# Windowed attention and a two-layer network on one core: transfers merged, and the ordered list given a limit of eight DMAs in flight

## The chip, the cores and the metric

One core of a Trainium2 chip runs the program. The metric is the device time in microseconds of one execution. The kernel before took 888.34 us as the median of three runs (885.73, 888.34 and 893.09).

## What is computed

```python
def _attn_ref(q, k, v):                    # 8 batches, 8 heads, 576 positions, 64 wide
    scores = scale * np.matmul(q, k.transpose(0, 1, 3, 2))
    mask = (rel >= 0) & (rel < 64)         # each position sees itself and the 63 before it
    ...                                    # softmax: minus the maximum, exp, over the sum + 1e-09
    return np.matmul(attn, v)

def _moe_ref(x, w_in, w_out):              # x: 4608 x 512, w_in: 512 x 2048, w_out: 2048 x 512
    h = x @ w_in
    g = np.maximum(0.01 * h, h)
    return g @ w_out
```

The attention's result, laid out as 4608 rows of 512, is the x of the network.

## The kernel before

**Tiles.** Queries are taken in blocks of 64 positions and two blocks at a time, called a pair, m = 0 to 35. A pair has scores of 128 keys by 2 x 512 columns, in two halves j = 0 and 1. The network runs over chunks of 512 rows. All products use values split into two parts (a high part in the matmul's own precision and the remainder), and three matmuls of 128 x 128 by 128 x 512 for each product, which are the parts of TensorE's work that the profile shows as m, h, acc, y and z.

**Stages.** First the string ORDER lists pairs 0 to 7, the conversion of the weights and the first products, word by word. The rest is built as a list of entries by op(engine, us, function, what it waits for, rank, lag, land). The function arrange then walks that list like a scheduler: each engine takes, among its entries whose predecessors have ended by the planned times, the one with the lowest rank, and the order that comes out is the order in which the instructions are issued. The planned times serve for nothing else. Everything on an engine runs in that order, so an instruction that waits holds all that stand behind it on its engine.

After ORDER come chunk products with tiles h and acc (early_first, early_second; lines 880 and 889), then three rounds s = 0, 1, 2. A round has a first product in seven half-size products (m, line 1058) and a second product: for s = 0 in the plain form (y, line 1083), for s = 1 and 2 again in seven half-size products (z, line 1121). In between them the attention of pairs 8 to 35 goes on, up to about 630 us.

**One late pair.** attend(m) loads q, k and v by DMAs that ScalarE issues (lines 161, 165 and 169), makes the scores on TensorE (line 272), adds the mask on VectorE, takes the maximum over the partitions on GpSimd (line 672), subtracts it, takes exp on ScalarE and sums over the partitions on GpSimd (line 675) into late_o. normalise(m) brings the sums into 128 x 8 numbers by two small DMAs (late_c, line 686), adds 1e-9 on ScalarE (690), inverts them on VectorE (694), writes them to HBM (rows, 697), and reads them back spread over the partitions (late_r, 710): half j's row of 512 goes to partitions 64 j to 64 j + 63. The product with V is on TensorE (722), the multiplication by late_r on VectorE (733) into late_n, and keep_of (736) writes that to x_rows in HBM. x_build (830, 835, 854, 857) reads two pairs back and makes the inputs of m.

**DMAs.** GpSimd issues those that fill a ring of four weight tiles (fill, line 1042); SyncE and ScalarE issue all others. Each of SyncE's and ScalarE's DMAs is given one of eight semaphores, by turns over both engines in the order of the list, and the engine that issues it first waits until the DMA that had the semaphore before has landed. No entry of the list says so: it is added when the program is built. The planned time of such an entry ends with its landing (land) only for those that wait for it.

**Stored weights.** split stores the single-precision copy of each half tile in w_single (line 241); store (632) puts the split parts into w_first and w_second. prepare(n, f) reads two singles, makes sums and differences of them on VectorE (979), splits these (982, 985) and stores them (989, 992): for n = 0 into w_first, for n = 1 into w_second, which holds eight blocks for the second products. In the second product y, high and low (1073, 1076) split one 128 x 512 tile of the activations at a time into one of four places; in z, wide_high and wide_low (1103, 1107) split 128 x 1024.

Of the kernel before, what the change touches and what calls it, by code (L numbers as in the profile page):

```python
# [24 lines left out]
P = 128  # L25
# [13 lines left out]
PACE = 2  # L39
EARLY = 20  # L40
FIRST_LATE = 14
# [61 lines left out]
def band_attention_ffn(ctx: ExitStack, tc: tile.TileContext, qT, kB, vW, vL, w_in, w_out, eye_mask, out, outT):  # L103
# [37 lines left out]
    qs = [const.tile([P, UNITS, NP, QB], F32, name=f"q{i}") for i in range(2)]  # L141
    ks = [const.tile([P, UNITS, NP, QB], F32, name=f"k{i}") for i in range(2)]
# [16 lines left out]
    def load_q(m, queue=nc.sync):  # L159
        if m < NU // 2:  # L160
            queue.dma_start(q_of(m), qT[m])

    def load_k(m, queue=nc.sync):
        if m < NU // 2:
            queue.dma_start(k_of(m), kB[m])
# [24 lines left out]
    w_single = dram.tile([2 * FT, P, 512], F32, name="w_single")  # L190
    w_first = dram.tile([P, half * 7 * 512], F32, name="w_first")
    w_second = dram.tile([P, 8 * half * 512], F32, name="w_second")
    second_at = w_second.rearrange("p (k f c) -> p k f c", k=8, f=half)
# [45 lines left out]
    def split(n):  # L239
        nc.scalar.copy(flat(parts(n)[0]), singles[n])  # L240
        nc.scalar.dma_start(w_single[n], singles[n])
# [238 lines left out]

    def idle(n):
# [14 lines left out]
    nc.scalar.dma_start(k_of(0), kB[0])  # L496
# [21 lines left out]
    def load(fn, *after, rank=1.0, us=0.5, land=4.0):  # L518
        return op("SP", us, fn, *after, rank=rank, land=land)

    def bulk(fn, *after, rank=1.0):
        return op("ACT", 0.45, fn, *after, rank=rank, lag=1.5, land=6.0)

    def arrange():
# [9 lines left out]
        order = []  # L534
        while any(waiting.values()):
            best = None
            for e, xs in waiting.items():
                if xs:
                    t = max(free[e], min(r for r, _ in xs))
                    if best is None or t < best[0]:  # L540
                        best = t, e
            t, e = best
            r, x = min((y for y in waiting[e] if y[0] <= t), key=lambda y: (y[1]["rank"], y[1]["n"]))
# [50 lines left out]
    def g_pair(n):  # L594
        t = pairs_of_g[n % 2] if n % 4 < 2 else own(("g", n // (2 * FT)), F32R)[:, n % 2]
        return t[:, 0], t[:, 1]

# [14 lines left out]
    for name in late.split():  # L612
# [3 lines left out]
        if kind == "raw":  # L616
            o["raw"] = bulk(partial(fetch_w, n), weights_of.get(n - 3, {}).get("join"), rank=0.2)
# [12 lines left out]

    def store(to, f, *cut):
        nc.sync.dma_start(to, both[f][cut])

    stored = []
    for f in turn_of:
        near, far = f % half, f // half
        for a, k in ((0, 0), (256, 4)) if far == 0 else ((256, 5),):
            to = first_at(near, k).rearrange("p (i c) -> p i c", i=2)
            stored.append((f, partial(store, to, f, slice(None), slice(2), slice(a, a + 256))))
        for a in range(2):  # L640
            to = second_at[:, (0, 2)[far] + (6, 2)[far] * a, near].rearrange("p (i c) -> p i c", i=2)
            stored.append((f, partial(store, to, f, slice(None), slice(2, 4), slice(256 * a, 256 * a + 256))))


# [50 lines left out]

    def rows_of(m):
# [11 lines left out]
    def spread_of(m, j):  # L708
        row = rows[m : m + 1, 512 * j : 512 * j + 512]
        nc.sync.dma_start(later["r"][64 * j : 64 * j + 64], row.broadcast_to([64, 512]))  # L710
# [20 lines left out]
    def product_of(m):  # L731
        x = by_unit(done_of(m)) if early(m) else turned(probs[m, "v"])
        nc.vector.tensor_tensor(by_unit(done_of(m)), x, turned(later["r"]), ALU.mult)
# [16 lines left out]
    at = {}  # L750

    def attend(m, gate):

        o, late = at.setdefault(m, {}), 0.0 if early(m) else 0.5
        before, two, three = (at.get(m - i, {}) for i in (1, 2, 3))
        if m > PAIRED:
# [3 lines left out]
            o["v"] = bulk(partial(load_v, m, nc.scalar), before["X1"])  # L760
# [3 lines left out]
        o["S"] = op(  # L764
            "PE", 1.0, partial(scores_of, m), o.get("q"), o.get("k"), before.get("E1"), before.get("E0"), three.get("take"), *takes, s_free,
# [3 lines left out]
        for j in range(2):  # L769
            free = (three.get("V"), three.get(f"A{j}"))  # L770
            o[f"E{j}"] = op("DVE", ONE, partial(shield_of, m, j), o["S"], *(() if held else free), gate, before.get("E1"), rank=0.8 + late)
            o[f"C{j}"] = op("ACT", ACTS, partial(copy_of, m, j), o[f"E{j}"], *free, rank=0.5 + late) if held else o[f"E{j}"]
        for j in range(2):
            o[f"P{j}"] = op("POOL", 1.95, partial(max_of, m, j), o[f"C{j}"], before.get(f"B{j}"), rank=0.5 + late)
            o[f"B{j}"] = op("DVE", ONE if held else TWO, partial(minus_of, m, j), o[f"P{j}"], rank=0.8 + late)
            o[f"X{j}"] = op("ACT", ACTS, partial(exp_of, m, j), o[f"B{j}"], rank=0.8 + late)
        for j in range(2):
            o[f"A{j}"] = op("POOL", 3.5, partial(add_of, m, j), o[f"X{j}"], before.get(f"c{j}"), rank=0.4 + late)
            o[f"c{j}"] = load(partial(compact_of, m, j), o[f"A{j}"], two.get("rows"), rank=0.3 + late)

    def normalise(m):

        late = 0.0 if early(m) else 0.5
# [3 lines left out]
        guard = op("ACT", 0.22, partial(guard_of, m), o["c0"], o["c1"], rank=0.8 + late, lag=0.3 + 6 * late)  # L787
        o["I"] = op("DVE", 0.25, partial(inverse_of, m), guard, rank=0.4 + late)
        o["rows"] = load(partial(rows_of, m), o["I"], rank=0.3 + late)
        for j in range(2):  # L790
            if m + 2 in at:
                at[m + 2][f"c{j}"]["after"].append(o["rows"])
        spread = [load(partial(spread_of, m, j), o["rows"], before.get("Y"), rank=0.3 + late) for j in range(2)]
        if early(m):
            free = [after["E1"], before.get("take"), o["I"]]
# [6 lines left out]
        o["Y"] = op("DVE", TWO if early(m) else ONE, partial(product_of, m), *spread, o.get("take"), o["V"], *kept, rank=0.8 + late, lag=0.3 + 6 * late)  # L802
        if m < UPC // UNITS * LEAD:
            hi = op("ACT", ACTS, partial(high_early, m), o["Y"], *x2_free, rank=0.8 + late)
            o["kept"] = [op("DVE", TWO, partial(low_early, m), hi, rank=0.8 + late)]
# [9 lines left out]
    def x_build(s, n, xt_of, xt_free, x_free):  # L815

        urge, wait = (1.4, 2.6) if s else (0.2, 0.2)
# [11 lines left out]
        def fetch(i):  # L829
            nc.sync.dma_start(xt_of()[0][:, 512 * i : 512 * (i + 1)], x_rows[m + i])  # L830

        got = [load(partial(fetch, i), *at[m + i]["kept"], *xt_free, rank=urge) for i in range(2)]
# [69 lines left out]
    def reload_of(c):  # L902
        t = stage[c] = place("xb", F32, 2) if c else place("xa1", F32)
        for i in range(4 if c else 2):
            nc.sync.dma_start(t[:, 512 * i : 512 * (i + 1)], sums.pop((c, i)))

    def early_out(c, i):
# [3 lines left out]
        else:  # L911
            (nc.scalar.copy if i % 2 else nc.vector.tensor_copy)(o, acc[c, i])
        nc.sync.dma_start(out[c * CH + i * P : c * CH + (i + 1) * P, :], o)
# [4 lines left out]
    def second_step(n):  # L918
# [5 lines left out]
        if n in ends:  # L924
            evicted[c] = []
            for i in range(4):
                engine = "DVE" if c == 1 or c == 0 and i < 2 or i % 2 == 0 else "ACT"
                evicted[c].append(op(engine, 0.75, partial(early_out, c, i), seconds[n][i], *reloads[c], rank=0.1))

    for n, (c, f) in enumerate(walk):  # L930
# [16 lines left out]
        if n in ends:  # L947
            reloads[c] = [load(partial(reload_of, c), first, s_free, rank=0.1)] if c < 2 else [first]
# [18 lines left out]
    def prepare(n, f, at, hurry, *freed):  # L967
# [399 lines left out]
```

## Time and profile before

| what | value |
|---|---|
| median of three runs | 888.34 us |
| the profiled execution | 888.97 us |
| its span, first to last instruction | 887.2 us |
| granted TensorE clock, mean | 0.987 |
| TensorE busy | 853.5 us, 96% of the span |
| VectorE busy | 631.6 us, 71% |
| ScalarE busy | 376.0 us, 42% |
| GpSimd busy | 364.2 us, 41% |
| moved by DMA | 227.08 MB, mean 256 GB/s |

Busy time is the union of an engine's instructions; those that only issue a DMA or wait are not in it. In the rows of the profile PE is TensorE, PEld its weight loads, DVE VectorE, ACT ScalarE, POOL GpSimd and SP SyncE; ACTq and SPq stand for the issuing of a DMA on these engines. A name such as L1058 is a line of the kernel before. Behind a row of instructions "[5.91 <-DVE gs L900]" says how long the engine sat idle before them and what ended that.

### The profile page before, as it was taken

Reading aid. Unit: us, or ns where it says so; the run is one execution under the profiler, and the core shown is the slowest. Engines: PE = TensorE matmul, PEld = TensorE weight load, DVE = VectorE, ACT = ScalarE, POOL = GpSimd, SP = SyncE. Lnnn points to the kernel's source line nnn. Section 1 sums busy time; section 2 is a strip of 40 time slices with the busy share of each in tenths; the row PEclk is TensorE's granted clock in tenths of the full one; section 3 lists DMA queues with packets and bytes.
Section 4 is the critical chain, followed back from the end, with each engine's and each line's share of the span. In section 5 each row is a group of like instructions: output and inputs, shape, how many; then the busy total and the mean of one; then the engine's idle time right before and its main releaser. Section 6 shows DMA issues by size and latency. Waiting matters only on the chain.

```text
span 887.2 us, 16927 instructions
## 1 busy us (share of the span) xinstructions
PE 853.5 (96%) x6778; PEld 690.0 (78%) x6778; DVE 631.6 (71%) x891; ACT 376.0 (42%) x620; POOL 364.2 (41%) x218
## 2 busy tenths in 40 slices
PE   8999999999999997999999899989999999999998
PEld 5776888888777776888887678767888888888886
DVE  7889885768579864875776989466578864545863
ACT  4655554333333333544453534253354523334431
POOL 5323000958768720677776777663000100000000
PEclk9999999999999998999999999989999999999999
DMA  9875876786899997799999998976856776666662
GB/s 342 265 233 184 275 219 240 234 302 207 276 292 336 314 317 273 245 299 356 309 295 317 295 300 266 344 235 207 276 195 214 236 242 210 194 191 197 199 222 87
DMA packets 103742, 227.08 MB, mean 256 GB/s; under 512 B 17008, under 2 KB 47856, under 8 KB 94704
## 3 DMA queue, kind: packets, MB, share of 16 engines
q0 software_dynamic: 14432, 90.18, 31.5%
q10 hardware_dynamic: 41712, 77.31, 26.3%
q1 hardware_dynamic: 47520, 58.51, 20.3%
q8 instruction: 53, 0.87, 0.4%
q14 instruction: 25, 0.20, 0.1%
HBM read 168.59 MB, written 57.26 MB: 255 GB/s over the span
## 4 chain that ended last, share of the span: by engine, by line
PE 48%; DMA 12%; DVE 9%; issue 3%; ACT 1%; SPq 1%; ACTq 0%; POOL 0%; DVEq 0%
PE m L1058 25%; PE z L1121 17%; DMA w_second<-p 2%; DMA late_r<-rows 2%; DMA w_second<-pspare 2%; DMA rows<-late_c 2%; DMA x_rows<-late_n 1%; PE y L1083 1%; PE acc L889 1%; DMA p<-x_rows 1%; PE s L272 1%; PE o L722 1%; DMA outT<-p 1%; DVE p L835 1%; DVE gs L1076 1%
## 5 line engine op out<-in xcount | busy, mean ns | idle before, releaser
L1058 PE MATMUL m<-pfew,p 128*128 128x512 f32 x720 | 171.5, 393 | 0.8 <-DVE pxa L1067 0.7
L1058 PEld LDWEIGHTS m<-pfew,p 128*128 128x128 f32 x720 | 134.8, 189 | 30.2 <-DVE pxa L1067 1.1
L1042 POOL DMA_DIRECT2D p<-w_second x44 | 26.3, 597 | 143.0 <-PE z L1121 98.8
L889 PE MATMUL acc<-p,gs 128*128 128x512 f32 x324 | 79.8, 394 | 0.0
L1042 POOL DMA_DIRECT2D p<-w_first x42 | 22.8, 542 | 134.0 <-PE m L1058 78.6
L1058 PE MATMUL m<-pxb,p 128*128 128x512 f32 x288 | 72.1, 397 | 5.0 <-ACT p L1070 5.0
L672 POOL PARTITION_ALL_REDUCE g<-late_f x20 | 37.0, 1894 | 96.1 <-DVE late_f L657 71.6
L675 POOL PARTITION_ALL_REDUCE late_o<-late_f x20 | 65.5, 3283 | 20.5 <-ACT late_f L683 12.3
L1067 DVE TENSOR_TENSOR p<-m,pxa 128x512 f32<-128x512 f32 x60 | 41.3, 688 | 41.9 <-PE m L1058 41.6
L1067 DVE TENSOR_TENSOR pxa<-m,pxa 128x512 f32<-128x512 f32 x60 | 41.3, 689 | 41.0 <-PE m L1058 38.0
L889 PEld LDWEIGHTS acc<-p,gs 128*128 128x128 f32 x324 | 60.1, 188 | 13.0
L1070 ACT ACTIVATE p<-p 128x512 f32<-128x512 f32 x60 | 37.9, 631 | 74.2 <-DVE p L1067 74.1
L1058 PEld LDWEIGHTS m<-pxb,p 128*128 128x128 f32 x288 | 54.4, 191 | 17.3 <-ACT p L1070 5.4
L880 PE MATMUL h<-pxa,p 128*128 128x512 f32 x228 | 58.4, 405 | 5.9 <-DVE gs L900 5.9
L675 POOL PARTITION_ALL_REDUCE late_o<-late_e x18 | 58.9, 3292 | 12.5 <-ACT late_e L683 8.0
L675 POOL PARTITION_ALL_REDUCE late_o<-e x18 | 58.8, 3285 | 8.2 <-ACT e L683 5.7
L1121 PE MATMUL z<-gs,p 128*128 128x512 f32 x240 | 57.6, 389 | 0.0
L880 PEld LDWEIGHTS h<-pxa,p 128*128 128x128 f32 x228 | 43.9, 195 | 16.5 <-DVE gs L900 7.2
L1083 PE MATMUL y<-gs,p 128*128 128x512 f32 x192 | 48.7, 406 | 3.8 <-issue 3.8
L1121 PEld LDWEIGHTS z<-gs,p 128*128 128x128 f32 x240 | 45.0, 188 | 9.4
L1121 PE MATMUL z<-third,p 128*128 128x512 f32 x216 | 51.9, 389 | 0.0
L1121 PE MATMUL z<-pxa,p 128*128 128x512 f32 x216 | 51.9, 389 | 0.0
(192 smaller groups left out, 1710.2 us busy)
## 6 DMA issues: line engine op xcount, KB each, us to landing
p<-w_second POOLq DMA_DIRECT2D x44, 1024.0 KB, 5.3
p<-w_first POOLq DMA_DIRECT2D x42, 1024.0 KB, 6.1
w_single<-w ACTq DMA_DIRECT2D x32, 256.0 KB, 4.4
w_second<-pspare ACTq DMA_DIRECT2D x16, 512.0 KB, 6.0
raw<-w_out ACTq DMA_DIRECT2D x15, 512.0 KB, 4.4
k<-kB ACTq DMA_DIRECT2D x28, 256.0 KB, 4.7
raw<-w_in ACTq DMA_DIRECT2D x14, 512.0 KB, 4.3
more_v<-vL ACTq DMA_DIRECT2D x14, 512.0 KB, 4.4
```

Of the source, the lines that this page charges most:

```text
L272: nc.tensor.matmul(ps[j][t, c : c + QB], k[i][s, p], q[s, w, p], start=not begun and (not more or (w, p) == (0, 0)), stop=not begun and no ...
L672: nc.gpsimd.partition_all_reduce(most_of(j), e_of(m)[:, j], P, ReduceOp.max)
L675: nc.gpsimd.partition_all_reduce(sum_of(j), e_of(m)[:, j], P, ReduceOp.add)
L722: nc.tensor.matmul(ps[64 * j : 64 * j + 64, c : c + QB], v[:, 2 * p + j], e_of(m)[:, j, c : c + QB], start=True, stop=True,)
L880: nc.tensor.matmul(ps, a[:, k, :], b[:, k], start=i == 0, stop=i == len(terms) - 1)
L889: nc.tensor.matmul(acc[c, i], a[:, i * P : (i + 1) * P], b, start=begin and k == 0, stop=n in ends and k == 2)
L1042: nc.gpsimd.dma_start(to, of)
L1058: nc.tensor.matmul(tiles[b], w[:, 256 * i + 128 * kt : 256 * i + 128 * kt + 128], x_part(OF_X[k], j, kt), start=begin and c == 0, stop=c = ...
L1067: nc.vector.tensor_tensor(to(), tiles[b], x(), ALU.add)
L1070: nc.scalar.activation(to(), to() if b is None else tiles[b], AF.Prelu, alpha=0.01)
L1083: nc.tensor.matmul(tiles[i], a, b, start=f == 0 and k == 0, stop=f == FT - 1 and k == 2)
L1121: nc.tensor.matmul(tiles[b + i], a, x, start=begin and f == 0 and c == 0, stop=f == half - 1 and c == 2, skip_group_check=not begin,)
```

## The change

1. arrange now keeps eight landing times (LANES): an entry of SyncE or ScalarE with a landing can't start in the plan before the earliest of them. Planned landings become 4.8 and 6.5 us in place of 4.0 and 6.0, and several ranks change. The DMAs that send results (early_send, send) and the single reloads become entries of their own.
2. q and k lie in one input, qk, and from pair 10 on come in one load of 128 x 1024 (load_qk).
3. The inverse sums of a pair are spread by one DMA in place of two (spread_of), and x_build reads its two pairs by one.
4. Only the singles of w_in are stored. w_second now holds the split parts of w_out by f, stored by one DMA for each f in place of two; the sums and differences have a tensor of their own, w_sums. prepare(1, f) reads both parts from w_second and adds them (whole_of, a 128 x 1024 addition more on VectorE), and waits for these stores and for x_build(0). In z the factors that aren't sums are read from w_second in pieces of 256 numbers.
5. For pair 19 alone (direct) the inverse is taken on the whole tile: two additions of 1e-9 on ScalarE, one reciprocal of 128 x 512 on VectorE; its two small DMAs, the write and the spread are gone.
6. In y the activations are split 128 x 1024 at a time into one of two places, by wide_high and wide_low.

```diff
+LANES = 8
+DIRECT_FROM = 19
...
+    def load_qk(m):
+        nc.scalar.dma_start(both_qk[m % 2], qk[m])
...
     def split(n):
         nc.scalar.copy(flat(parts(n)[0]), singles[n])
-        nc.scalar.dma_start(w_single[n], singles[n])
+        if n % 2 == 0:
+            nc.scalar.dma_start(w_single[n // 2], singles[n])
...
-        order = []
+        order, landed = [], [0.0] * LANES
+
+        def begins(ready, x):
+            return max(ready, landed[0]) if x["land"] and x["engine"] != "POOL" else ready
...
-                    t = max(free[e], min(r for r, _ in xs))
+                    t = max(free[e], min(begins(*y) for y in xs))
...
+            if x["land"] and e != "POOL":
+                landed.pop(0)
+                landed.append(x["end"])
...
+    def whole_guard_of(m, j):
+        half_of = slice(64 * j, 64 * j + 64)
+        nc.scalar.activation(sum_of(0)[half_of], sum_of(j)[half_of], AF.Copy, bias=1e-9)
+
+    def whole_inverse_of(m):
+        nc.vector.reciprocal(sum_of(0), sum_of(0))
...
-    def spread_of(m, j):
-        row = rows[m : m + 1, 512 * j : 512 * j + 512]
-        nc.sync.dma_start(later["r"][64 * j : 64 * j + 64], row.broadcast_to([64, 512]))
+    def spread_of(m):
+        nc.sync.dma_start(later["r"], rows[m].rearrange("(j c) -> j c", j=2)[:, None].broadcast_to([2, 64, 512]))
...
-            if m > PAIRED + 1:
-                o["q"] = bulk(partial(load_q, m, nc.scalar), two["S"], rank=0.5 + late)
-            o["k"] = bulk(partial(load_k, m, nc.scalar), before["S"], rank=0.2 + late)
...
+        if m > PAIRED + 1:
+            o["k"] = bulk(partial(load_qk, m), before["S"], rank=0.2 + late)
...
-        got = [load(partial(fetch, i), *at[m + i]["kept"], *xt_free, rank=urge) for i in range(2)]
+        got = [load(fetch, *at[m]["kept"], *at[m + 1]["kept"], *xt_free, rank=urge, land=5.0)]
...
-            to = prep(0)[:, i::2] if n else prep(0)[:, 2 * i : 2 * i + 2]
-            nc.scalar.dma_start(to, w_single[2 * (f + half * i) + n].rearrange("p (k c) -> p k c", k=2))
+            if n:
+                to = tile_of()[:, 1024 * i : 1024 * (i + 1)].rearrange("p (j c) -> p j c", j=2)
+                nc.scalar.dma_start(to, w_second[:, f::half, 512 * i : 512 * (i + 1)])
+            else:
+                nc.scalar.dma_start(prep(0)[:, 2 * i : 2 * i + 2], w_single[f + half * i].rearrange("p (k c) -> p k c", k=2))
+
+        def whole_of():
+            nc.vector.tensor_tensor(prep(0), prep(0), prep(1), ALU.add)
...
+    used_last[0] = used_last[0] + x_done
+    for f in range(half):
+        prepare(1, f, 0, OUT_PREP + 0.1 * f, *used_last[0])
...
+    def factor(of, f):
+        if isinstance(of, int):
+            return w_sums[:, of, f : f + 4].rearrange("p f c -> p (f c)")
+        begin, a = of
+        return w_second[:, begin + f : begin + f + 4].rearrange("p f (i c) -> p (f i) c", i=2)[:, :, a : a + 256]
...
-                hi = op("ACT", ACTS, partial(high, q, partial(g_part, t, f)), made[t, f], *free, rank=0.2)
-                split_of[t, f] = op("DVE", TWO, partial(low, q, partial(g_part, t, f)), hi, rank=0.2)
+                    hi = op("ACT", 1.07, partial(wide_high, s, 2 * (q % 2), t, j, p), made[t, f], made[t, f + 1], *free, rank=0.2)
+                    lo = op("DVE", 1.6, partial(wide_low, s, 2 * (q % 2), t, j, p), hi, rank=0.2)
```

In all, ScalarE issues 165 DMAs in place of 207 and SyncE 262 in place of 322; GpSimd's 86 and TensorE's matmuls stay.

Three places of the order, word for word. The words in brackets are what a row waits for: DMAHW0 to DMAHW7 are the eight semaphores, the others are engines.

**ScalarE, the end of the chunk products.** L894 and L897 before (L933 and L936 now) take the tile h out of TensorE's bank and make its high part, which the products acc need. Before:

```order
L897 CAST gs0_81<-h2_7_3448 128x512 [waits PE_49,Activation_49]
L690 ACTIVATE late_c1_1789<-late_c1_1789 128x8 [waits DMAHW0_49]
L976 DMA pspare_18_1804<-w_single_96 128x2x256 [waits DMAHW7_49,DMAHW2_49]
L976 DMA pspare_18_1804<-w_single_96 128x2x256 [waits DMAHW3_49]
L992 DMA w_first_97<-p14_24_2971 128x1536 [waits DMAHW4_49]
L992 DMA w_first_97<-p14_24_2971 128x512 [waits DMAHW7_49]
L894 ACTIVATE h2_8_3490<-h2_8_3490 128x512 [waits DVE_49,PE_49]
L992 DMA w_first_97<-p15_23_2883 128x1536 [waits DMAHW1_49]
L992 DMA w_first_97<-p15_23_2883 128x512 [waits DMAHW4_49]
L854 CAST pxb_27_3457<-p12_26_3088 128x2x256 [waits DMAHW6_49]
L897 CAST gs1_82<-h2_8_3490 128x512 [waits PE_49,Activation_49]
```

Now:

```order
L170 DMA qk1_84<-qk 128x1024 [waits DMAHW5_49,PE_49]
L936 CAST gs0_81<-h2_7_3399 128x512 [waits PE_49,Activation_49]
L933 ACTIVATE h2_8_3479<-h2_8_3479 128x512 [waits DVE_49,PE_49]
L893 CAST pxb_27_3408<-p12_25_3083 128x2x256 [waits DMAHW3_49]
L893 CAST pfew_28_3418<-p12_25_3083 128x256
L672 COPY late_f_1766<-s20_0_3423 128x512 [waits DVE_49]
L936 CAST gs1_82<-h2_8_3479 128x512 [waits PE_49,Activation_49]
```

Six DMAs stood between the high parts of h2_7 and h2_8, and none does now; the reads of w_single for these tiles stand ahead of h2_6, and the stores behind h2_10.

**VectorE, pair 19.** L939 makes the remainder of h (L900 before), and TensorE's acc waits for it; L752 (L733 before) is the multiplication by the spread inverse. Now:

```order
L1035 TENSOR_TENSOR p15_23_2855<-p15_23_2855 128x256 [waits DVE_49] x2
L713 RECIPROCAL late_o0_1769<-late_o0_1769 128x512 [waits Activation_49]
L939 TENSOR_TENSOR gs0_81<-h2_5_3286,gs0_81 128x512 [waits PE_49,Activation_49]
L752 TENSOR_TENSOR late_n_1767<-late_n_1767,late_r_1768 128x4x2x64 [waits DMAHW5_49,DMAHW4_49]
L752 TENSOR_TENSOR late_n_1767<-late_n_1767,late_o0_1769 128x4x2x64 [waits DMAHW4_49,DVE_49,Activation_49]
L939 TENSOR_TENSOR gs1_82<-h2_6_3349,gs1_82 128x512 [waits PE_49,Activation_49]
```

The whole-tile reciprocal stands straight ahead of the remainder of h2_5; pair 19's product stands two remainders from there, and before it stood between those of h2_9 and h2_10.

**SyncE, the spread.** Before:

```order
L632 DMA w_second_98<-pfew_3_87 128x2x256 [waits DMAHW0_49]
L697 DMA rows_1586<-late_c1_1789 128x8 [waits DMAHW3_49,DMAHW5_49,DMAHW2_49,DVE_49]
L632 DMA w_second_98<-pfew_3_87 128x2x256
L686 DMA late_c0_1788<-late_o0_1786 64x1x8 [waits DMAHW5_49,Pool_49]
L736 DMA x_rows_1587<-late_n_1784 128x512 [waits DMAHW6_49,DVE_49]
L710 DMA late_r_1785<-rows_1586 64x512 [waits DMAHW7_49,DMAHW2_49]
L710 DMA late_r_1785<-rows_1586 64x512 [waits DMAHW0_49]
```

Now:

```order
L498 DMA w_second_96<-p6_5_87 128x1024 [waits DMAHW7_49]
L716 DMA rows_1571<-late_c1_1772 128x8 [waits DMAHW0_49,DVE_49]
L498 DMA w_first_95<-p7_6_88 128x2x256 [waits DMAHW2_49]
L695 DMA late_c0_1771<-late_o0_1769 64x1x8 [waits DMAHW3_49,Pool_49]
L755 DMA x_rows_1572<-late_n_1767 128x512 [waits DMAHW5_49,DVE_49]
L498 DMA w_first_95<-p7_6_88 128x2x256 [waits DMAHW6_49]
L695 DMA late_c0_1771<-late_o1_1770 64x1x8 [waits DMAHW7_49,Pool_49]
L728 DMA late_r_1768<-rows_1571 128x1x512 [waits DMAHW0_49]
```

Two transfers to 64 partitions each have become one to 128, whose source is two rows, each repeated 64 times; and w_second comes in one store of 1024 numbers per partition in place of two of 2 x 256.

More of the change, by code (lines that the diff above doesn't have):

```diff
@@ L102, in band_attention_ffn @@
 @with_exitstack
[L103 removed]
+def band_attention_ffn(ctx: ExitStack, tc: tile.TileContext, qk, vW, vL, w_in, w_out, eye_mask, out, outT):
     nc = tc.nc
@@ L629, in band_attention_ffn @@
     stores = {f: [] for f in range(FT)}
[L631 to L642, printed above, removed]
+    stored = [(f, fn) for f in turn_of for fn in stores_of(f)]
     def scores_of(m):
@@ L900, in low_of, with reload_of @@
         nc.vector.tensor_tensor(pair_at[n][:, 1], h_of[n], pair_at[n][:, 0].bitcast(F32), ALU.subtract)
[L902 to L905, printed above, removed]
+    def reload_of(c, i):
+        if c not in stage:
+            stage[c] = place("xb", F32, 2) if c else place("xa1", F32)
+        nc.sync.dma_start(stage[c][:, 512 * i : 512 * (i + 1)], sums.pop((c, i)))
     def early_out(c, i):
@@ L947, in band_attention_ffn @@
         if n in ends:
-            reloads[c] = [load(partial(reload_of, c), first, s_free, rank=0.1)] if c < 2 else [first]
+            reloads[c] = [first]
+            for i in range((2, 4, 0)[c]):
+                reloads[c].append(load(partial(reload_of, c, i), first, s_free, rank=0.1))
         if n == half + 1:
```

183 lines of the change are left out of this document (109 added, 74 removed).

## The prediction

> **What bounds the kernel now.** First the page's head, and the table of stages, whose columns are the stretch, each engine's busy time with its instructions, the granted clock, the DMA engines' mean busy share and GB/s.
>
> ```profile
> span 887.2 us, 16927 instructions
> ...
> PE 853.5 (96%) x6778; PEld 690.0 (78%) x6778; DVE 631.6 (71%) x891; ACT 376.0 (42%) x620; POOL 364.2 (41%) x218
> ```
>
> ```profile
> 240.00:320.00 80.00, 75.21 (x719) 59.82 (x718) 65.62 (x88) 30.94 (x56) 55.46 (x23) 1.00 0.95 314
> 320.00:340.00 20.00, 14.09 (x83) 11.16 (x82) 8.71 (x16) 6.76 (x13) 1.24 (x3) 0.89 1.00 364
> 340.00:480.00 140.00, 140.00 (x1349) 113.94 (x1348) 96.81 (x137) 60.33 (x105) 92.97 (x52) 0.99 0.91 295
> 480.00:500.00 20.00, 18.82 (x167) 15.24 (x167) 17.50 (x23) 10.35 (x20) 14.09 (x8) 1.00 0.97 307
> 500.00:520.00 20.00, 16.22 (x144) 12.60 (x144) 16.03 (x19) 8.42 (x17) 13.52 (x8) 0.83 0.92 284
> 560.00:600.00 40.00, 34.93 (x312) 27.18 (x311) 22.51 (x34) 14.59 (x27) 25.38 (x15) 0.91 0.87 288
> 620.00:880.00 260.00, 260.00 (x1149) 215.29 (x1148) 165.63 (x191) 103.78 (x133) 23.82 (x45) 1.00 0.65 209
> ```
>
> TensorE is the bound: it idles 887.2 - 853.5 = 33.7 us. From 620 to 880 us it never stops, so nothing can be won there. The idle time that a change of order can touch lies between 240 and 620 us: 4.8 us up to 320, then 5.9, 1.2, 3.8 and 5.1 us in the rows shown. After the larger gaps the granted clock falls too (0.89, 0.83, 0.91). The waits of TensorE between 240 and 620 us name what ended the gaps:
>
> ```profile
> PE h L880 <- DVE gs L900: 7.4, 2, 5.9
> PE m L1058 <- ACT p L1070: 5.0, 1, 5.0
> PE y L1083 <- issue: 3.8, 1, 3.8
> ```
>
> Three gaps make 14.7 us. The timeline shows the first, and the chain of waits (its last two rows here) what stood behind it:
>
> ```profile
> 306.62 2.88 PE L880 MATMUL h<-pxa,p 128*128 128x512 f32 x12
> 334.55 0.87 ACTq L992 DMA_DIRECT2D w_first<-p  x2
> 335.99 0.58 ACT L897 CAST gs<-h 128x512 fp32r<-128x512 f32 x1
> 336.60 0.69 DVE L900 TENSOR_TENSOR gs<-h,gs 128x512 fp32r<-128x512 f32 x1 [7.87 <-ACT gs L897]
> 337.35 5.43 PE L880 MATMUL h<-pxa,p 128*128 128x512 f32 x12 [5.91 <-DVE gs L900]
> 321.19 13.34 DMA w_second<-p
> 334.55 0.33 ACTq L992
> ```
>
> ScalarE could issue its store L992 only at 334.55 us, when SyncE's store of w_second, on its way for 13.34 us, had landed. The two move unrelated data; what they share is one of the eight semaphores. The high part of h (L897) stood behind that issue, then its remainder on VectorE, then TensorE, 5.91 us. The twelve matmuls behind the gap took 5.43 us where twelve undisturbed ones take 2.88: 2.55 us more for the clock. The third gap is of the same kind:
>
> ```profile
> 569.41 9.16 DMA outT<-p
> 572.67 1.66 PE L1058 MATMUL m<-pfew,p 128*128 128x512 f32 x6
> 578.59 0.34 ACTq L165 DMA_DIRECT2D k<-kB  x1
> 579.50 0.63 ACT L1070 ACTIVATE p<-p 128x512 f32<-128x512 f32 x1
> 580.68 2.93 PE L1058 MATMUL m<-pxb,p 128*128 128x512 f32 x6 [4.99 <-ACT p L1070]
> 583.40 6.34 PE L1058 MATMUL m<-pfew,p 128*128 128x512 f32 x24
> 596.31 5.60 PE L1058 MATMUL m<-pfew,p 128*128 128x512 f32 x24
> ```
>
> The load of k waited for the store of outT, and L1070, which frees TensorE's bank, stood behind it: 4.99 us of idle time, and (2.93 - 1.66) + (6.34 - 5.60) = 2.0 us of clock. The second gap isn't of this kind:
>
> ```profile
> 502.82 2.98 DVE L857 TENSOR_TENSOR pxb<-p,pxb 128x512 fp32r<-128x512 f32 x1
> 506.32 0.67 DVE L1086 COPY p<-y 128x512 f32<-128x512 f32 x1
> 507.10 4.18 PE L1083 MATMUL y<-gs,p 128*128 128x512 f32 x9 [3.78 <-issue]
> ```
>
> Between the halves of y the bank waits for VectorE's copy L1086, late behind one long addition.
>
> **The change part by part.** *The ordered list with eight landings, and 102 fewer DMAs* (529 to 427 on the two engines). This goes at the first and third gap. In the new order no DMA of ScalarE stands between h2_7 and h2_8, where six stood. I take both gaps as gone, with their clock: 5.91 + 2.55 + 4.99 + 2.0 = 15.45 us. What is late next there is the rest of the idle time between 240 and 600 us, in small pieces; I leave it and the second gap as they are. Bounds: nothing gained (the waits move to another place), and all of 240 to 620 us gained, which is 20.8 us idle (4.8 + 5.9 + 1.2 + 3.8 + 5.1) and 2.55 + 2.0 us of clock, with 2.0 more at the second gap (nine matmuls in 4.18 us, at twelve in 2.88 they take 2.2), 27.4 us: 861.6 us.
>
> *Pair 19's reciprocal.* The trace has it for 4 and for 8 columns:
>
> ```profile
> L694 DVE RECIPROCAL late_c<-late_c 128x8 f32<-128x8 f32 x28 | 5.4, 193 | 10.3 <-ACT late_c L690 10.3
> L373 DVE RECIPROCAL sm<-sm 128x4 f32<-128x4 f32 x16 | 2.6, 167 | 0.1
> ```
>
> That is (193 - 167) / 4 = 6.5 ns a column, so an estimated 0.19 + 504 x 0.0065 = 3.5 us for 512. Behind it on VectorE stands the remainder of h2_5, for which acc waits. The cover is the twelve matmuls of h2_6, the twelve of the acc before and the pair's product with V, 2.88 + 2.88 + 1.1 = 6.9 us, more than 3.5 + 0.7. I take 0; without cover it costs up to 3.5 us of idle time and 2.5 us of clock.
>
> *prepare(1, f)* gets an addition of 128 x 1024, eight times. Nearest row: the addition of that size in the same tile, L985.
>
> ```profile
> L985 DVE TENSOR_TENSOR pspare<-pspare 128x1024 fp32r<-128x1024 f32 x12 | 17.6, 1468 | 2.5 <-ACT pspare L982 2.4
> L1076 DVE TENSOR_TENSOR gs<-p,gs 128x512 fp32r<-128x512 f32 x16 | 24.3, 1516 | 3.9 <-ACT gs L1073 3.9
> L1107 DVE TENSOR_TENSOR gs<-p,gs 128x1024 fp32r<-128x1024 f32 x20 | 24.8, 1241 | 9.7 <-ACT gs L1103 9.7
> ```
>
> 8 x 1.47 = 11.7 us of VectorE. *y* gives time back: 32 remainders at up to 1.52 us become 16, whose nearest row is z's 1.24 us for twice the width, so more than 11.7 us go. The next pair has 24 matmuls (5.4 us) in which to be made, and takes 1.05 + 1.24 us. I take 0 for the two, bounds -3.8 us (the second gap goes) and +11.7 us.
>
> *q and k in one load, fewer stored singles, x_build's one read, z's reads in pieces:* hidden, since no row of TensorE's waits names one of these loads, and GpSimd's ring fills wait for z, not z for them:
>
> ```profile
> POOL p L1042 <- PE z L1121: 118.5, 24, 5.5
> ```
>
> If the pieces halve a fill's speed it still has three tiles of z ahead of it. I take 0 for these.
>
> *The spread in one DMA of 256 KB.* Its rows:
>
> ```profile
> late_r<-rows SPq DMA_DIRECT2D x56, 128.0 KB, 5.3
> q1 hardware_dynamic: 47520, 58.51, 20.3%
> 302.83 1.10 SPq L710 DMA_DIRECT2D late_r<-rows  x2
> 309.29 0.68 DVE L733 TENSOR_TENSOR late_n<-late_n,late_r 128x512 f32<-128x512 f32 x1
> ```
>
> Two landings of 5.3 us side by side become one; between issue and product lie 6.5 us in this case. If it goes over all 16 DMA engines like its parts, the price is nothing. But its source starts with a dimension of 2, and no transfer of before has one below 64 there, so the trace can't say how it is spread. The Trainium skill speaks against it: "DMA: Bandwidth & Descriptors", section "Why a DMA increments its semaphore by 16 and not by 1", says that a DMA runs on the largest number of engines, at most 16, that divides the slowest dimension of both its sides. By that it is 2 here, where the halves had 16, and the sum would be the second rival's below instead of a gain; no run here shows it.
>
> **The sum.** From the profiled execution's 888.97 us (span 887.2 and 1.8 around it, 0.6 above the median): 888.97 - 15.45 = 873.5 us.
>
> **The rivals.** *The waits move.* It isn't enough that the plan knows of eight landings if its landing times are too short. For it speaks that they are 4.8 and 6.5 us, while the two that did the harm took 13.34 and 9.16; against it, 102 fewer DMAs to wait for. One gap of the size of each then comes back elsewhere: 873.5 + 15.45 = 889 us, range 881 to 900.
>
> *The merged spread runs on few engines*, the one that ends slower. The price: queue q1 (packets, MB, share of 16 engines) moved 58.51 MB in 20.3% of 16 x 887.2 us, which is 49.2 us of one engine for a MB, so the spread's 0.262 MB takes 12.9 us of engine time. On 16 engines that is 0.8 us each, on two 6.45, for 27 pairs 27 x 5.65 = 152 us more on these two. A transfer that is spread over all lands when the slowest engine is done. How much room they have:
>
> ```profile
> 160.00:620.00 460.00, 438.55 (x4139) 351.95 (x4138) 334.73 (x441) 183.69 (x328) 301.86 (x151) 0.98 0.88 286
> ```
>
> 0.12 x 460 = 55 us. So up to 97 us don't fit, and 873.5 + 97 = 970 us is the top. At the bottom stands the latency alone, with the engine time fitting in: 5.6 us more for 27 products, of which the order's distance takes most; about 20 us, 893. Middle 932 us. It decides as soon as the spread lands later than the order leaves room for, 6.5 us in the pair shown: then VectorE stands at the product, and TensorE behind it. For it speaks the share of 0.88, which leaves little room on any two engines; against it, that the halves with 64 in front landed in 5.3 us, so a front shorter than 128 alone hasn't cost anything so far.
>
> **How the numbers follow.** Gaps go, 861 to 884 us: 0.48. Spread on few engines, 893 to 970: 0.36. Waits move, 881 to 900: 0.16. The forecast is the first, 873.5 us. The range that holds 8 in 10 has to reach into the second: 861 to 962 leaves out its top and the first's bottom, about 0.1 together. One per cent, which is what a measurement of this kernel can tell (the three runs lie 0.8% apart), is 879.5 to 897.2 us: faster 0.41, the first case without its top; within it 0.19, the rest of the first and most of the third; slower 0.40, nearly all of the second and a little of the third.
>
> **What would show it.** Right: no wait of TensorE above 2 us between 240 and 600 us, clock 1.00 in those slices, late_r landing in 5 to 7 us. The second rival: late_r lands in over 9 us, other landings of SyncE grow with it, and VectorE idles until DMA late_r. The third: ScalarE's issues still held by landings of stores. Wrong beyond these would be a stall at pair 19's reciprocal or in y at the splits.

## The result, and the profile after

The changed kernel takes 958.98 us (median; 953.64 to 966.29) where the kernel before takes 889.97 us beside it: a ratio of 1.078, interval 1.070 to 1.087. The profiled execution took 958.28 us. The time lies near the top of the range and belongs to the second rival; the forecast of 873.5 us is missed by 85 us and has the wrong sign.

Head and engines of the page of the changed kernel, with its lines on packets, the queue of SyncE and the issues of the spread:

```profile
span 956.5 us, 16749 instructions
...
PE 873.3 (91%) x6778; PEld 704.5 (74%) x6778; DVE 609.5 (64%) x883; ACT 374.7 (39%) x605; POOL 365.3 (38%) x218
...
DMA packets 98531, 226.79 MB, mean 237 GB/s; under 512 B 14743, under 2 KB 45591, under 8 KB 88983
...
q1 hardware_dynamic: 39654, 58.24, 18.1%
...
late_r<-rows SPq DMA_DIRECT2D x27, 256.0 KB
```

TensorE has the same 6778 matmuls, but idles 956.5 - 873.3 = 83.2 us, 49.5 more than before; the other 19.8 us are longer matmuls, for the clock (0.960 on average, 0.987 before). VectorE, whose share fell from 71% to 64%, isn't short of time. The stages, in the stretches shown of before (the columns are the same):

```profile
240.00:320.00 80.00, 65.38 (x621) 51.87 (x621) 40.29 (x61) 19.96 (x37) 48.30 (x21) 0.89 0.74 248
320.00:340.00 20.00, 18.54 (x193) 14.84 (x192) 11.24 (x12) 11.26 (x20) 5.61 (x2) 1.00 0.46 159
340.00:480.00 140.00, 123.86 (x1027) 99.92 (x1026) 85.37 (x130) 52.77 (x93) 76.12 (x44) 0.94 0.81 273
480.00:500.00 20.00, 12.04 (x131) 9.52 (x130) 9.68 (x13) 5.29 (x8) 5.67 (x4) 0.83 0.56 181
620.00:880.00 260.00, 242.59 (x1177) 198.74 (x1176) 155.96 (x200) 97.29 (x140) 45.14 (x51) 0.96 0.73 222
160.00:620.00 460.00, 401.64 (x3785) 321.44 (x3784) 270.59 (x375) 159.13 (x275) 271.93 (x135) 0.94 0.77 256
```

The last row is the one to read against the rival's argument: in the stretch of the pairs the mean share of the DMA engines fell from 0.88 to 0.77, while the waits for two kinds of DMA grew. The longest waits of VectorE and ScalarE for a DMA, and two of TensorE's for VectorE (engine and line, awaited engine and line; total us, times, longest):

```profile
DVE late_n L752 <- DMA late_r<-rows: 122.5, 16, 12.7
ACT late_c L699 <- DMA late_c<-late_o: 40.0, 5, 11.4
PE o L740 <- DVE late_n L752: 15.2, 3, 7.7
PE m L1117 <- DVE p L1126: 11.5, 3, 9.1
```

The product's wait for the spread is now 122.5 us. In all of the kernel before it was this:

```profile
DVE late_n L733 <- DMA late_r<-rows: 1.2, 1, 1.2
```

The wait for late_c is for a DMA of 2 KB, which nobody edited: some of the small transfers of the same chain of a pair are late too. A piece of the chain of waits, around two pairs (start, duration, what):

```profile
388.53 18.82 DMA late_c<-late_o
...
412.70 15.54 DMA late_r<-rows
...
428.27 0.70 DVE late_n L752
...
429.42 20.24 DMA late_r<-rows
```

These two spreads take 15.5 and 20.2 us from issue to landing, where the halves took 5.3. By the semaphores in the trace all 27 take 7.0 to 20.5 us, 12.0 us in the middle. The semaphores also show what held late_c: 14 of the 16 landings that raise its semaphore came within 5.7 us of the issue, the last two at 401.96 and 407.35 us. The spread that was issued just ahead of it, at 386.70 us, has only two such landings, at 401.76 and 407.18 us. So the parts of late_c that came late stood behind the two parts of the spread. The next spread can be issued only after the product has read the tile, so the spreads stand end to end. TensorE's end of it, from the timeline (idle time before the row in brackets): VectorE stands at the product until 449.7 us, the addition L1126 that empties a bank of m is behind it, and TensorE waits.

```profile
451.09 2.93 PE L1117 MATMUL m<-pfew,p 128*128 128x512 f32 x6 [9.05 <-DVE p L1126]
```

### The profile page after: what moved, and what is told of

Same layout as the page of the kernel before. It is cut to its first block, busy times and chain, and to the rows that moved or that the text cites. A ratio compares the mean times of both kernels' runs of the same rounds, so it can differ in the third digit from the quotient of the medians.

```text
span 956.5 us, 16749 instructions
## 1 busy us (share of the span) xinstructions
PE 873.3 (91%) x6778; PEld 704.5 (74%) x6778; DVE 609.5 (64%) x883; ACT 374.7 (39%) x605; POOL 365.3 (38%) x218
## 3 DMA queue, kind: packets, MB, share of 16 engines
q1 hardware_dynamic: 39654, 58.24, 18.1%
## 4 chain that ended last, share of the span: by engine, by line
PE 49%; DMA 33%; DVE 11%; issue 3%; POOL 2%; ACT 1%; SPq 1%; ACTq 0%; DVEq 0%; POOLq 0%
PE z L1180 16%; PE m L1117 13%; DMA late_r<-rows 12%; DMA late_c<-late_o 7%; PE acc L928 4%; PE h L919 4%; PE h L431 4%; PE acc L467 4%; DMA rows<-late_c 3%; DMA w_second<-p 3%; DMA w_sums<-pspare 2%; PE s L278 1%; DMA w_single<-w 1%; POOL late_o L684 1%; DMA pxb<-sum 1%
## 5 line engine op out<-in xcount | busy, mean ns | idle before, releaser
L1117 PE MATMUL m<-pfew,p 128*128 128x512 f32 x720 | 177.8, 403 | 13.4 <-DVE p L1126 11.2
L1117 PEld LDWEIGHTS m<-pfew,p 128*128 128x128 f32 x720 | 138.9, 195 | 45.2 <-DVE p L1126 12.1
L684 POOL PARTITION_ALL_REDUCE late_o<-e x18 | 58.9, 3293 | 33.9 <-ACT e L692 15.5
L1126 DVE TENSOR_TENSOR p<-m,pxa 128x512 f32<-128x512 f32 x60 | 41.3, 689 | 41.6 <-PE m L1117 41.3
L1137 PE MATMUL y<-gs,p 128*128 128x512 f32 x192 | 50.6, 412 | 12.5 <-DVE p L1126 8.0
L1126 DVE TENSOR_TENSOR pxa<-m,pxa 128x512 f32<-128x512 f32 x60 | 41.3, 688 | 31.1 <-PE m L1117 25.9
L752 DVE TENSOR_TENSOR late_n<-o,late_r 128x512 f32<-128x512 f32 x16 | 10.9, 682 | 76.1 <-DMA late_r<-rows 76.1
L919 PE MATMUL h<-pxa,p 128*128 128x512 f32 x228 | 55.6, 394 | 3.6 <-DVE gs L939 3.6
L1137 PEld LDWEIGHTS y<-gs,p 128*128 128x128 f32 x192 | 37.0, 198 | 22.2 <-DVE p L1126 8.1
```

Of the source, the lines that this page charges most:

```text
L684: nc.gpsimd.partition_all_reduce(sum_of(j), e_of(m)[:, j], P, ReduceOp.add)
L919: nc.tensor.matmul(ps, a[:, k, :], b[:, k], start=i == 0, stop=i == len(terms) - 1)
L1117: nc.tensor.matmul(tiles[b], w[:, 256 * i + 128 * kt : 256 * i + 128 * kt + 128], x_part(OF_X[k], j, kt), start=begin and c == 0, stop=c = ...
L1126: nc.vector.tensor_tensor(to(), tiles[b], x(), ALU.add)
L1137: nc.tensor.matmul(tiles[i], a, b, start=f == 0 and k == 0, stop=f == FT - 1 and k == 2)
```

## The experiments

Times are medians; the ratio is to the kernel before on the same chip, whose median was 887.9 to 891.8 us.

| kernel | us | ratio | interval |
|---|---|---|---|
| changed kernel | 958.98 | 1.078 | 1.070 to 1.087 |
| two halves in one step of the list (two_spreads) | 868.56 | 0.976 | 0.971 to 0.982 |
| two halves, a step for each (two_entries) | 863.24 | 0.970 | 0.965 to 0.975 |
| the same version, run beside no_direct and land6 | 865.07 | 0.972 | 0.968 to 0.976 |
| two halves, 2 in front (halves_on2) | 968.65 | 1.083 | 1.076 to 1.090 |
| two halves, 4 in front (halves_on4) | 897.31 | 1.011 | 1.007 to 1.014 |
| two halves, 8 in front (halves_on8) | 869.07 | 0.981 | 0.977 to 0.984 |
| before, with the merged spread alone (before_merged) | 962.66 | 1.078 | 1.074 to 1.083 |
| before, with the limit of eight landings alone (before_lanes) | 881.40 | 0.991 | 0.987 to 0.994 |
| two_entries without that limit (no_lanes) | 873.85 | 0.985 | 0.982 to 0.988 |
| two_entries with all singles stored (all_singles) | 866.27 | 0.978 | 0.975 to 0.981 |
| two_entries without the whole-tile inverse (no_direct) | 871.53 | 0.980 | 0.976 to 0.985 |
| two_entries with a landing of 6.0 us in the plan (land6) | 865.26 | 0.973 | 0.969 to 0.977 |

**Undoing the merge.** The list of steps stays as in the changed kernel; only what the step issues is different.

```diff
-        nc.sync.dma_start(later["r"], rows[m].rearrange("(j c) -> j c", j=2)[:, None].broadcast_to([2, 64, 512]))
+        for j in range(2):
+            row = rows[m : m + 1, 512 * j : 512 * j + 512]
+            nc.sync.dma_start(later["r"][64 * j : 64 * j + 64], row.broadcast_to([64, 512]))
```

> The changed kernel with the same list of steps, but the step of the spread issues two DMAs of 128 KB (64 partitions each, source with 64 in front) instead of one of 256 KB with 2 in front. Theory (two DMA engines carry the merged spread): nearly all of the loss goes, and what is left is the rest of the change: 870 to 884 us, late_r lands soon enough that VectorE's wait at the product falls from 122 us to under 15. Rival A (the new order, the lanes or the other edits cost the time): 945 to 965 us, with the waits elsewhere. Rival B (half and half): 900 to 940 us.

868.56 us: 90 us less than the changed kernel, and 2.4% less than before. The page with the row of SyncE's queue, and the wait at the product:

```profile
span 866.7 us, 16808 instructions
...
PE 845.6 (98%) x6778; PEld 685.2 (79%) x6778; DVE 620.7 (72%) x883; ACT 374.7 (43%) x605; POOL 365.8 (42%) x218
...
DMA packets 99341, 226.80 MB, mean 262 GB/s; under 512 B 15552, under 2 KB 46400, under 8 KB 89792
...
q1 hardware_dynamic: 40464, 58.24, 20.1%
```

```profile
DVE late_n L754 <- DMA late_r<-rows: 6.1, 8, 1.4
```

One line made the loss; rival A falls. All that is left of the change is a gain, and a little larger than I had forecast.

With a step for each half in the list, as in the kernel before:

> The changed kernel with two steps for the spread in the list, one DMA each, as in the kernel before, so the planner gives each half a lane of its own. Theory (two engines): 868 to 884 us, within 6 us of the version that issues both halves in one step. Rival A (order and lanes cost the time): 945 to 965 us.

863.24 us, 0.970 of before. That is 5 us below the theory's range (868 to 884), and within the 6 us of the other version; rival A falls again. This version beats both kernels.

**The merge alone, in the kernel before.**

```diff
     def spread_of(m, j):
-        row = rows[m : m + 1, 512 * j : 512 * j + 512]
-        nc.sync.dma_start(later["r"][64 * j : 64 * j + 64], row.broadcast_to([64, 512]))
+        if j == 0:
+            nc.sync.dma_start(later["r"], rows[m].rearrange("(j c) -> j c", j=2)[:, None].broadcast_to([2, 64, 512]))
```

> The kernel before with one edit: of its two spread steps the first issues the merged DMA of 256 KB with 2 in front, the second nothing. Order and lanes stay otherwise. Theory (two engines): the loss comes without any other edit, 940 to 980 us, with VectorE waiting for late_r at the product for 70 to 130 us. Rival A (the other edits cost the time): 885 to 895 us, as before.

962.66 us, 71 us more than before, with the same wait:

```profile
DVE late_n L733 <- DMA late_r<-rows: 87.5, 16, 16.1
```

So the edit is enough for the loss as well as needed for it. Note that it ends at nearly the same time as the changed kernel, though the rest of the change is worth 23 us. That fits with the transfers, and no longer the order, setting the end; it is argued from the times alone.

**Size and number of DMAs against the dimension in front.** Two DMAs of 128 KB again, with the same bytes and packets of 2 KB, but the source written with a short dimension in front:

```diff
-            nc.sync.dma_start(later["r"][64 * j : 64 * j + 64], row.broadcast_to([64, 512]))
+            nc.sync.dma_start(later["r"][64 * j : 64 * j + 64], row[:, None].broadcast_to([2, 32, 512]))
```

> The changed kernel's order with two DMAs for the spread, but each source written with 2 in front (0-step 2, 0-step 32, 512) in place of 64: the same bytes, the same packets, the same number of DMAs as with two halves of 64 in front. Theory (the front dimension sets the number of engines, and the load on them is the price): if both halves fall on the same two engines, 945 to 970 us like the one merged DMA; if on four different ones, 900 to 930 us. The posts of 4 bytes fall by 54 x 14 against two halves of 64. Rival (one DMA of 256 KB or the lane plan is what costs): 870 to 884 us, no different from two halves of 64.

968.65 us, as bad as the merged one, so neither the 256 KB nor the single DMA is at fault. The number of packets below 512 bytes fell:

```profile
DMA packets 98585, 226.79 MB, mean 234 GB/s; under 512 B 14796, under 2 KB 45644, under 8 KB 89036
```

They tell how many engines took part. In the trace of two_spreads SyncE's 289 DMAs have 4624 packets of 4 bytes (posts), 16 each, and 16 landings raise the semaphore of each half; I take each post for one engine that carried a part. Here 15552 - 14796 = 756 = 54 x 14: each of the 54 halves has 14 posts fewer, 2 in place of 16. In the changed kernel SyncE's queue (q1) has 40464 - 39654 = 810 = 27 x 30 packets fewer than in two_spreads: 27 DMAs with 2 posts where 54 had 16.

Both halves run on the same two engines. They are issued 0.6 us apart, and by the semaphores the second lands 5.6 us behind the first in the middle of the 27 pairs, where with 64 in front it lands 0.7 us behind. The time, too, is that of the merged DMA, and not the 897 us that four engines take below.

Then 4 and 8 in front (broadcast to 4 x 16 and 8 x 8 rows):

> As the version with two halves of 2 in front, but 4 in front (0-step 4, 0-step 16, 512), in the order of the version with two halves of 64 in front (868.6 us). Theory (load on few engines against their free room): four engines take 27 x (3.23 - 0.81) = 65 us more each, by 12.9 us of engine time a pair; the free room is 0.11 x 380 us between 240 and 620 us and about 15 us before, 55 us, so some 10 us don't fit: 872 to 895 us. Rival (a short front costs by its latency alone, in proportion to its length): the 100 us between 868.6 and 968.7 fall to 3.23 - 0.81 over 6.45 - 0.81, 43 us: 905 to 917 us. Posts of 4 bytes on SyncE's queue: 3760 + 54 x 4 = 3976.

> As before it with 8 in front. Theory (load against room): 27 x 0.81 = 22 us more on eight engines, which fits in the room: 866 to 875 us. Rival (latency in proportion): 14 us, 880 to 886 us. Posts of 4 bytes on SyncE's queue: 3760 + 54 x 8 = 4192.

```profile
DMA packets 98693, 226.79 MB, mean 255 GB/s; under 512 B 14904, under 2 KB 45752, under 8 KB 89144
```

```profile
DMA packets 98909, 226.80 MB, mean 261 GB/s; under 512 B 15120, under 2 KB 45968, under 8 KB 89360
```

Posts again as many as the dimension: 14904 - 14796 = 54 x 2, 15120 - 14796 = 54 x 6. The times are 897.31 and 869.07 us. Against 868.56 with 16, eight engines cost nothing that can be told (the intervals of the two ratios overlap), four 29 us and two 100 us. For eight it is as the theory has it. For four both expectations miss: the theory had 872 to 895 us, by some 10 us that don't fit, the rival 905 to 917, by 43 us, and the 29 measured lie between. Load against room gives the shape, then, but not the size at four. The DMA engines' mean share (the last column but one) in the stretch in which the spreads are issued, for 2 engines (the changed kernel, whose last one begins at 690 us), 4, 8 and 16 (which are through at about 620 us):

```profile
160.00:690.00 530.00, 455.11 (x4129) 364.12 (x4128) 304.30 (x422) 179.14 (x309) 295.97 (x151) 0.93 0.76 251
```

```profile
160.00:620.00 460.00, 434.73 (x4124) 348.26 (x4122) 306.42 (x420) 177.40 (x307) 292.59 (x150) 0.99 0.86 288
```

```profile
160.00:620.00 460.00, 448.14 (x4201) 361.28 (x4200) 332.63 (x441) 186.73 (x320) 296.33 (x152) 0.99 0.88 299
```

```profile
160.00:620.00 460.00, 445.78 (x4208) 359.42 (x4207) 331.38 (x442) 186.50 (x320) 297.34 (x153) 1.00 0.88 300
```

By the queue's row of the changed kernel a MB takes 0.181 x 16 x 956.5 / 58.24 = 47.6 us of one engine, a spread of 0.262 MB 12.5 us, and 27 of them 337 us. Take these from the 16 engines' total, divide the rest evenly, and add the spreads to the few that carry them. Estimated busy time of the most loaded engines: on two, 0.76 x 530 - 337 / 16 + 337 / 2 = 550 us of 530, which is more than there is; on four, 459 of 460; on eight, 426; on sixteen, 405. By this estimate the price begins where these engines are full, while the mean of all 16 is 0.76 to 0.86. It is not shown: the profile has no row for one engine. GpSimd's fills, whose parts run on these engines as well, landed only about 1 us later in the changed kernel than in two_spreads (rows in the last section). So it may be enough that the transfers of SyncE's queue wait for the spread ahead of them on these two engines; no run tells the two apart.

**What the rest of the change is worth.** The limit of eight landings, taken out of the better version (LANES = 64 in place of 8):

> The version with two steps for the spread (863.2 us), with the planner's limit of eight landings out of reach (64 in place of 8); all else as there, the order comes out differently. Theory (the limit in the plan takes away the gaps that ScalarE's and SyncE's issues made): 873 to 882 us, with waits of TensorE behind a held-up issue again. Rival (the gain comes from fewer DMAs and new landing times, the limit adds nothing): 860 to 867 us.

873.85 us, 10.6 more than the 863.24 us of two_entries, and gaps of the known kind are back. The longest wait of TensorE, 5.7 us in y, is for a high part of ScalarE (L1163), which had idled 15.86 us until a spread had landed. For the second, shown here, ScalarE's load of more_v can be issued only when the load of qk has landed, L1130 stands behind it, and TensorE waits 4.95 us. Pieces of the chain, and TensorE's row:

```profile
550.53 13.60 DMA qk<-qk
564.13 0.02 issue
564.16 0.34 ACTq L174
564.49 0.05 issue
564.54 1.12 ACT p L1130 x2
```

```profile
565.71 2.69 PE L1118 MATMUL m<-pxb,p 128*128 128x512 f32 x6 [4.95 <-ACT p L1130]
```

The same limit put into the kernel before, alone (the function that orders the list starts a transfer only when the eighth before it has landed; landing times stay 4.0 and 6.0 us):

> The kernel before with the planner's limit of eight landings alone: its landing times stay 4.0 and 6.0 us, its 529 DMAs stay, only the order comes out differently. Theory (the limit is worth what its removal cost, 873.9 - 863.2 = 10.6 us, and takes the two gaps of 5.9 and 5.0 us): 874 to 882 us. Rival (with 102 DMAs more and landing times that are too short the limit helps little): 884 to 890 us.

881.40 us, 0.991: within the theory's range (874 to 882), at its upper end. The old gaps go, as it says, but others come, of 6.4 and 4.2 us. Behind the second stands a load that lands after 14 us where the plan has 6:

```profile
549.75 14.23 DMA k<-kB
563.98 0.04 issue
564.03 1.01 PE s L273 x25
```

So the limit alone brings 8 us of the 24 to 29 by which two_entries beats the kernel before; the rest needs the other edits beside it.

All singles stored (16 more DMAs of 256 KB that nobody reads):

```diff
-        if n % 2 == 0:
-            nc.scalar.dma_start(w_single[n // 2], singles[n])
+        nc.scalar.dma_start(w_single[n // 2 + FT * (n % 2)], singles[n])
```

> The version with two steps for the spread (863.2 us), but all 32 singles are stored, as in the kernel before; the 16 more are read by nobody. Theory (in the kernel before VectorE waited 2.4 us for stores of singles, and TensorE 3.4 us for VectorE, before 80 us): 865 to 870 us, with TensorE's waits for pxb back before 80 us. Rival (the stores are hidden): 861 to 865 us.

866.27 us: 3 us more than the first measurement of two_entries, with intervals that just touch, and 1 us more than the second, so hardly clear of noise. VectorE's wait for a stored single is back, as it stood in the kernel before (2.4 us there), and TensorE has lost 76.83 - 75.03 = 1.8 us of busy time before 80 us (rows of two_entries and of this one). These are single executions, and that of all_singles, of 872.84 us, is the slowest of its six:

```profile
DVE w L242 <- DMA w_single<-w: 1.7, 2, 1.4
```

```profile
0.00:80.00 80.00, 76.83 (x1018) 59.05 (x1019) 71.27 (x154) 48.84 (x91) 32.27 (x20) 1.00 0.76 249
```

```profile
0.00:80.00 80.00, 75.03 (x1011) 57.03 (x1011) 70.85 (x149) 47.50 (x89) 31.44 (x20) 1.00 0.82 271
```

Pair 19 through the compact tile like the others (DIRECT_FROM = 20), a truer landing time for the halves, and the version they are compared with:

> The version with two steps for the spread (863.2 us), with pair 19 through the compact tile and its DMAs like the others. Theory (the reciprocal of 3.35 us has cover, and the DMAs it saves were hidden): 860 to 867 us. Rival A (it frees the path at a crowded place): 868 to 875 us. Rival B (VectorE's 3.35 us delayed TensorE): 855 to 860 us.

> The version with two steps for the spread, with a landing time of 6.0 us in the plan for the two halves, as measured there, in place of 4.8. A try at a better version. Theory (a truer time sets the product later in the order and takes some of the 14 us of idle time): 857 to 862 us. Rival (the order is as good as it gets within such shifts): 862 to 868 us.

> The version with two steps for the spread once more, beside the other three on the same chip, so that differences under one per cent can be read: 861 to 866 us.

Without the whole-tile inverse it is 871.53 us against 865.07, so the inverse brings some 6 us: rival A, not my theory. Where they come from is not settled, since the order differs in many places; no wait of TensorE above 3 us appears or goes, and the idle time, 872.9 - 848.9 = 24.0 us against 859.6 - 847.4 = 12.2 in the profiled executions, lies in small pieces. The landing time changes nothing (865.26; the theory's 857 to 862 us fails). In land6 TensorE waits 6.0 us for L1130, behind a store of outT that landed after 11.81 us, and the time is the same all the same: one such gap doesn't by itself account for the 10.6 us of no_lanes.

## Why the prediction was wrong

**The failed step is the term "the spread in one DMA", taken at nothing.** It measured 958.98 - 868.56 = 90 us in the new order and 71 us in the old. The text had the price, up to 97 us, and the place: late_r lands after 7.0 to 20.5 us, 12.0 in the middle, the product waits, TensorE behind it, as the second rival says. What was wrong was the choice. I weighed "the halves with 64 in front landed in 5.3 us" against it, but 64 is no evidence on 2: what counts is on how many engines the front dimension can be dealt out: 64 and 8 give the same time here, 4 and 2 don't. The Trainium skill, "DMA: Bandwidth & Descriptors", section "Why a DMA increments its semaphore by 16 and not by 1", gives that number as the largest divisor, at most 16, of the slowest dimension of both sides; the posts of this case agree at each of the four values tried (2, 4, 8 and 64). It should have had the larger chance.

**The size of its price fits, in part by luck.** 873.5 + 97 = 970 us was the top, and the changed kernel ended at 959; the latency alone (893 us, the rival's bottom) is far too little. The price came from "engine time that doesn't fit in the room", with the mean share of all 16 engines as the load of the two. The same sum for four engines gave some 10 us where 29 were measured, so that it comes out so near for two isn't proof of it.

**The sum of the rest held, in part by luck:** 873.5 us forecast, 868.56 measured with the spread in halves, but by other terms. The gaps I named are gone: TensorE's longest wait is 2.9 us in two_spreads, and its idle time 866.7 - 845.6 = 21.1 us against 33.7; its busy time fell by 7.9 us, with the clock, where I had 4.55. Of the idle time I had 5.91 + 4.99 = 10.9 us going between 240 and 620 us; there only 365.78 - 358.55 = 7.2 us went, since other waits came. But the first stretch gave 76.95 - 71.89 = 5.1 us that I had at nothing (rows below, of before and of two_spreads), perhaps 1.8 of it from the stored singles, which I called hidden because TensorE's waits don't name them. They stood one engine further back: VectorE waited for the stores.

```profile
0.00:80.00 80.00, 71.89 (x983) 55.01 (x984) 67.28 (x144) 45.11 (x85) 30.75 (x20) 1.00 0.79 266
...
240.00:620.00 380.00, 358.55 (x3307) 287.59 (x3306) 277.07 (x374) 154.61 (x275) 240.47 (x127) 0.97 0.91 295
```

```profile
0.00:80.00 80.00, 76.95 (x1019) 59.25 (x1020) 71.73 (x155) 49.21 (x92) 32.38 (x20) 1.00 0.76 251
...
240.00:620.00 380.00, 365.78 (x3348) 294.92 (x3347) 278.07 (x377) 156.66 (x265) 232.51 (x127) 1.00 0.89 305
```

**Pair 19's inverse** took 3.35 us (estimated 3.5) and delayed nobody. But it wasn't worth nothing: some 6 us by no_direct. **prepare(1, f)**'s wide addition took 1.93 us, not 1.47, and no wait of TensorE names it.

```profile
L713 DVE RECIPROCAL late_o<-late_o 128x512 f32<-128x512 f32 x1 | 3.4, 3353 | 0.9 <-ACT late_o L710 0.9
L1032 DVE TENSOR_TENSOR pspare<-pspare 128x1024 f32<-128x1024 f32 x8 | 15.5, 1934 | 0.9 <-DMA pspare<-w_second 0.9
```

**"The waits move"** didn't decide: with the spread in halves TensorE's longest wait is 2.9 us. But it is no idle rival. It came in before_lanes and in land6, where the plan knows of the eight landings and some took 14.23 and 11.81 us.

## What to carry to other kernels

Two DMAs are not dearer than one if the one has 2 in front: before merging transfers, look at the outermost dimension of both sides, and keep it large: 64 and 8 were enough here, 4 and 2 were not. The mean share of all 16 engines doesn't show what a narrow transfer costs; it fell from 0.88 to 0.77 while the kernel lost 90 us. In a profile the sign is a low mean DMA share beside long landings, also of small transfers that nobody touched and that stand behind the narrow one in the same queue, and the count of packets below 512 bytes tells how many engines took part.

## What was unexpected of the hardware

Two different DMAs of 2 in front, to different halves of a tile, take the same two engines: the second lands 5.6 us behind the first, and the kernel takes 968.65 us, no better than with one DMA of twice the size. A 0-step dimension (a broadcast of 2 x 32 or 8 x 8 of the same row) counts as a front dimension like any other: 2, 4 and 8 gave 2, 4 and 8 posts.

And two engines are enough to hold up a transfer that runs on all 16. The load of 2 KB of late_c took 18.82 us in the piece of the chain above, because two of its 16 parts stood behind the spread. This goes for those that are issued behind a spread: in the middle late_c lands after 5.5 us in the changed kernel too, by the semaphores, and the longest took 20.2 us (12.3 in two_spreads). GpSimd's fills, which have a queue of their own, were held up little. Rows of the changed kernel, then of two_spreads (the last number is the landing):

```profile
p<-w_first POOLq DMA_DIRECT2D x42, 1024.0 KB, 6.8
p<-w_second POOLq DMA_DIRECT2D x28, 1024.0 KB, 7.7
```

```profile
p<-w_first POOLq DMA_DIRECT2D x42, 1024.0 KB, 5.6
p<-w_second POOLq DMA_DIRECT2D x28, 1024.0 KB, 6.8
...
late_c<-late_o SPq DMA_DIRECT2D x54, 2.0 KB, 5.6
```
